# A clamp in two operations on POOL, low bits on POOL, and an order planned anew

## The chip, the cores and the metric

The kernel runs on one core of one Trainium2 chip. The metric is the device time of one execution in microseconds (us), lower is better. Engines are named as the profile names them: PE is TensorE, PEld its weight load, DVE is VectorE, ACT is ScalarE, POOL is GpSimd, SP the engine that issues most transfers.

## What is computed

Attention over 4 batches, 8 heads, 576 positions of 64 elements, and then two feed-forward layers over its 2304 rows of 512. In the attention a score that lies more than tau below its row's maximum is left out.

```python
scores = scale * np.matmul(q, k.transpose(0, 1, 3, 2))
thresh = np.max(scores, axis=-1, keepdims=True) - tau
scores = np.where(scores >= thresh, scores, -1000000000.0)
attn = np.exp(scores - max); attn = attn / (sum + 1e-09)
x = attn @ v                                  # rows of 512
x = (np.maximum(x @ w_in, 0.0) ** 2) @ w_out  # 512 -> 2048 -> 512
h = x @ w2_in
y = (h * np.tanh(log1p(exp(h)))) @ w2_out
```

The weights arrive as 64-bit floats, the rest as 32-bit.

## The kernel before, in words

The kernel is written as a list of small operations. Each has the engines on which it may run with an estimated time for each (S, A, P, V, T: SP's queue, ScalarE, POOL, VectorE, TensorE), the buffers that it reads and writes, and a due time. A planner (`Plan`) then walks through time, gives each operation an engine and a place in that engine's queue, and the kernel is emitted in this order. For an operation that may run on several engines, `forwards` compares for each engine the time when it would end there, plus a constant for the engine (`BIAS`). Several passes backwards and forwards set the due times anew (`fbi`). `PAR` holds the planner's settings: due times of the tiles (`blk`, `ahead`, `start`, `off`), which transfers may be issued by which engine (`won` for the weights, one entry for each layer), and how many of the weight places that stand empty at the start are lent to attention and to the conversion (`ex`, `exo`: `cr` raw weights, `cw` converted ones, `sc` scores, `raw` inputs, `pd` turned scores).

The work has three parts. Attention runs first, unit by unit: TensorE makes scores, VectorE evacuates them with their minimum or maximum (line 783), ScalarE takes the exponential (line 806), VectorE masks and sums (line 817) and normalises (lines 831, 834), TensorE multiplies with the values. The first layer takes nine tiles of 256 rows, each as soon as attention has them, and so runs among the attention. The second layer follows.

A weight is converted before its use, in 128 x 512 pieces, 32 for each layer: `load` brings the 64-bit words; `size` (line 462, ScalarE) takes the upper word's magnitude; `rest` (lines 470, 472) takes the top three bits of the lower word, on ScalarE by a multiplication and rounding or on VectorE by a shift; `clamp` (line 465, VectorE or POOL) limits the magnitude; `shift` (line 477) joins both; the sign comes back either by `sign` (line 483, VectorE) or by `factor` and `times` (lines 489, 492: ScalarE, then POOL or VectorE). Which way is taken, `sp` says: for layer 0 the first of a weight column's four pieces goes by `factor` and `times`. Then `to_hi` (line 511) rounds to TensorE's reduced 32-bit form and `to_lo` (line 521) subtracts to get the rest. The MLP's activations go through `to_hi` and `to_lo` as well.

The planner has a term for VectorE and POOL meeting: `port` is the time up to which one of them is occupied by an operation marked `two`, and the next such operation is made longer by 0.6 (VectorE) or 0.15 (POOL) of what is left.

Of the kernel before, what the change touches and what calls it, by code (L numbers as in the profile page):

```python
# [15 lines left out]
U32 = mybir.dt.uint32  # L16
# [11 lines left out]

PAR = dict(
    on=dict(),  # L30
    won=("S", "S"),
    land=1.8,
    lag=1.045,
    turns=("h", "s1"),
    kv=(("nat0", "V1"), ("f1", "nat1"), ("KT1", "f0"), ("V0", "KT0")),
    cd=(-103.359, 8.066, -43.099),
    urg=-3.138,
    rawt=19.607,
    kinds="dddd",
    cgen=0.081,  # L40
    split=(),
    ex=dict(cw=1, cr=22, raw=4, pd=2, sc=4),
    exo=("pd", "cw", "sc", "raw", "cr"),
    blk=list((22.378, 87.527, 172.036, 247.705, 353.772, 474.186, 575.438, 769.06, 852.156)),
    tb2=207.373,
    down2=-110.768,
    sp=(1, 0),
    off=(115.794, 85.638, 120.96, -226.354, 75.139, 25.769, -102.917, -5.246),
    ahead=(13.309, 135.862, 0.835, -119.128, 12.338, 42.57, 40.034, 91.863, 160.78, 84.376),
    start=-49.931,  # L50
    area=dict(sc=("x0", "x1"), hl=("x2",)),
    jobahead=19.218,
    fbi=8,
    stay=-23.036,
    kinds2="ssss",
)

# [21 lines left out]
class Plan:  # L79
# [3 lines left out]


    TABLE = 1.3
    BIAS = {"V": 2.329, "A": -28.964, "P": 2.606, "S": 0.46}
    SHARE = 0.8
    FIRST = 1.0
    TICK, ENTRY = 3.4133, 1.275

    def __init__(self):
# [105 lines left out]
    def forwards(self, succ):  # L197
# [3 lines left out]
        free = dict.fromkeys(engs, 0.0)  # L201
        queue = dict.fromkeys("APS", 0.0)
        cand = {e: {} for e in engs}
        port = 0.0
        table, half = None, False
        work = {}

# [12 lines left out]
        while count < len(ops):  # L220
            best = None
            for e in engs:
                c = cand[e]
                if not c:
                    continue
                t = max(free[e], min(c.values()))
                if best is not None and t >= best[0]:
                    continue
                now = sorted((ops[n].due, n) for n, at in c.items() if at <= t)
                pick = None  # L230
                for _, n in now:
                    o = ops[n]
                    if len(o.opts) > 1:
                        bias = self.BIAS
                        mine = t + o.opts[e] + bias[e]
                        better = False
                        for a, d in o.opts.items():
                            if a != e:
                                ahead = sum(
                                    ops[m].opts[a] for m, at in cand[a].items()  # L240
                                    if at <= t and ops[m].due < o.due and len(ops[m].opts) == 1
                                )
                                if max(free[a], cand[a][n]) + ahead + d + bias[a] < mine - 1e-9:
                                    better = True
                        if better:
                            continue
                    pick = n
                    break
                if pick is None:

                    later = [at for at in c.values() if at > t]
                    later += [f for f in free.values() if f > t]
                    if not later:
                        continue
                    free[e] = stop = min(later)
                    if best is None or stop < best[0]:
                        best = (stop, e, None)
                    continue
                if e == "A" and ops[pick].tab is not None and table is not None and table not in ops[pick].tab:
                    same = [n for _, n in now if ops[n].tab is None or table in ops[n].tab]  # L260
                    same = [n for n in same if ops[n].due < ops[pick].due + 4.0 and len(ops[n].opts) == 1]
                    if same:
                        pick = same[0]
                if e == "T" and ops[pick].half != half:
                    same = [n for _, n in now if ops[n].half == half and ops[n].due < ops[pick].due + PAR["stay"]]
                    if same:
                        pick = same[0]
                if best is None or t < best[0]:
                    best = (t, e, pick)
            t, e, pick = best  # L270
            if pick is None:
                continue
            o = ops[pick]
            for a in o.opts:
                cand[a].pop(pick, None)
            o.eng, o.start = e, t
            dur = o.opts[e]
            if o.load is None and (e == "P" or e == "V" and o.two):
                dur += (0.15 if e == "P" else 0.6) * max(0.0, port - t)
                port = max(port, t + dur)  # L280
            if e == "A" and o.tab is not None:
                if table is None or table not in o.tab:
                    dur += self.TABLE
                    table = o.tab[0]
            if e == "T":
                dur += 0.1 * (half and not o.half)
                half = o.half
            free[e] = t + dur if e != "T" else self.stream(work, t, dur)
            o.end = free[e]
            if o.load is not None:  # L290
                off, last, z = o.load
                t += PAR["land"] + (0.15 if e == "P" else 0.0) + (self.FIRST if t < 8.0 else 0.0)
                to = max(t, queue[e])
                other = max(f for a, f in queue.items() if a != e)
                z += min(z, max(0.0, other - to)) * self.SHARE
                o.end = queue[e] = max(t + off + last, to + z)
            count += 1
            for s in succ[pick]:
                left[s] -= 1
                if not left[s]:  # L300
                    offer(ops[s])
# [4 lines left out]
def attention_moe_moe_kernel(ctx: ExitStack, tc: tile.TileContext, q, k, v, tau, w1i, w1o, w2i, w2o, out):  # L306
    nc = tc.nc
# [55 lines left out]
    def rot(*places):  # L363
# [8 lines left out]
        "q1": (dict(S=0.75, P=0.8), 0.0, 0.4, 0.4), "q2": (dict(S=1.45, P=1.4), 0.62, 0.19, 0.65),  # L372
        "w": (dict(S=0.6, P=0.75, A=0.45), 0.0, 1.8, 1.75), "n3": (dict(S=2.3, P=2.0), 1.24, 0.9, 1.6),
        "n2": (dict(S=1.45, P=1.35), 0.62, 0.5, 1.4),
        "xs": (dict(S=0.72, P=0.65), 0.0, 0.36, 0.36), "tail": (dict(S=1.3, P=1.3), 0.6, 0.19, 0.38),
        "xl": (dict(S=0.63, P=0.56), 0.0, 0.55, 0.5), "x2": (dict(S=0.6, P=0.56), 0.0, 0.75, 0.7),
        "xr": (dict(S=0.45, P=0.56), 0.0, 0.64, 0.64), "out": (dict(S=0.45, A=0.45), 0.0, 0.65, 0.65),
        "out4": (dict(S=2.6), 1.8, 0.2, 0.8), "turn": (dict(S=1.55), 0.0, 1.3, 1.2),
# [45 lines left out]
    def weights(layer, kind, j, due, places, wplaces):  # L424
# [5 lines left out]
        for half in range(2):  # L430
# [23 lines left out]
            def lower(raw=raw):  # L454
                return raw()[:, :, 0]
# [6 lines left out]
                nc.scalar.activation(out=w(), in_=upper().bitcast(F32), func=AF.Abs, scale=W_SCALE)  # L462

            def clamp(e, w=w):
                VEC[e].tensor_scalar(out=w(), in0=w(), scalar1=W_MAX, scalar2=None, op0=ALU.min)


            def rest(e, lower=lower):
                if e == "A":
                    nc.scalar.activation(out=lower(), in_=lower().bitcast(U32), func=AF.Copy, scale=0.93 * 2.0 ** -29)  # L470
                else:
                    nc.vector.tensor_scalar(
                        out=lower(), in0=lower(), scalar1=29, scalar2=None, op0=ALU.logical_shift_right
                    )
# [18 lines left out]

            dma(load, "w", w=[raw], due=due - 12, on=PAR["won"][layer])
            op({"A": 0.56}, size, r=[raw], w=[w], due=due - 4)
            op({"A": 0.56, "V": 0.34}, rest, x=[raw], due=due - 3.5 + O_CV, two=True)
            op({"V": 0.34, "P": 1.45}, clamp, x=[w], due=due - 3 + O_CV, two=True)
            op({"V": 0.6}, shift, r=[raw], x=[w], due=due - 2 + O_CV, two=True)
            if 2 * kind + half < PAR["sp"][layer]:
                op({"A": 0.56}, factor, x=[raw], due=due - 1.9 + O_CV)  # L500
                op({"P": 1.24, "V": 0.6}, times, r=[raw], x=[w], due=due - 1.8 + O_CV, two=True)
            else:
                op({"V": 0.6}, sign, r=[raw], x=[w], due=due - 1.9 + O_CV, two=True)
            to_hi(w, hi, part, due - 1 + O_CV)
# [2 lines left out]
    def to_hi(src, dst, part, due):  # L507
# [6 lines left out]
            else:  # L514
                nc.vector.tensor_copy(out=o, in_=i)

        op({"A": 0.52, "V": 0.34, "P": 0.6}, fn, r=[src], w=[dst], due=due, two=True)

    def to_lo(src, hi, lo, part, due):
        def fn(e):  # L520
            VEC[e].tensor_tensor(out=part(lo), in0=src(), in1=f32(part(hi)), op=ALU.subtract)  # L521

        op({"V": 0.6, "P": 1.24}, fn, r=[src, hi], w=[lo], due=due, two=True)


    x_dr = [dbuf(f"xdr{n}", [128, 2, 512], F32) for n in range(NB)]
# [299 lines left out]
    def head(p, g, hh, u, ex, due):  # L826
# [19 lines left out]
            VEC[e].tensor_tensor(out=hl()[:, a:a + n], in0=ex()[:, z:z + n], in1=hl()[:, z:z + n], op=ALU.subtract)  # L846

        op({"A": 0.58, "V": 0.38}, high, r=[ex], w=[hl], due=due + 2.5 + O_HL, two=True)
        op({"V": 0.6, "P": 1.24}, lambda e: low(e, 640, 0, 512), r=[hl, ex], w=[hl], due=due + 3 + O_HL, two=True)
        op({"V": 0.14, "P": 0.3}, lambda e: low(e, 576, 512, 64), r=[hl, ex], w=[hl], due=due + 3 + O_HL, two=True)  # L850
        pt = sbuf(place("pt", "pt0", "pt1", "pt2"), [128, 9, 128], F16)
        transpose(pt, hl, [hl], [pt], due + 4 + O_HL)
# [317 lines left out]
    def second():  # L1170
# [10 lines left out]
        for i, n in enumerate((*range(NB - 2), NB - 1, NB - 2)):  # L1181
# [3 lines left out]
            for g in range(2):  # L1185
# [15 lines left out]
                    VEC[e].tensor_tensor(out=xo(), in0=xr(), in1=f32(xh()), op=ALU.subtract)  # L1201

                op({"A": 0.52, "V": 0.34, "P": 0.66}, hi, r=[xr], w=[xh], due=blkd - 6, two=True)
                op({"V": 0.6, "P": 1.24}, lo, r=[xr, xh], w=[xo], due=blkd - 5, two=True)
                hs.append(xh)
                os_.append(xo)
            x = View(hs), View(os_)
# [171 lines left out]
```

## Time and profile before

| what | us |
|---|---|
| median of 3 runs | 1057.93 |
| the three runs | 1058.05, 1057.93, 1055.40 |
| the profiled execution's own time | 1057.58 |
| its span, first to last instruction | 1055.8 |
| TensorE busy in the span | 1012.6 |
| VectorE, ScalarE, POOL busy | 742.9, 786.8, 119.6 |

The span is what the rows below divide up. The profile's line numbers are those of the code above. Busy times of TensorE are modelled, as its instructions overlap; idle time of an engine matters only where that engine is the bound.

### The profile page before, as it was taken

The numbers are of one execution on the slowest core, as the hardware profiler recorded it, in microseconds if no ns is written. First come the engines' busy times: TensorE is split into PE (matmuls) and PEld (weight loads), VectorE is DVE, ScalarE is ACT, GpSimd is POOL, SyncE is SP. The second block draws the span as 40 slices with busy tenths as digits, with TensorE's granted clock in tenths as the row PEclk, the third lists the DMA queues.
The fourth block names the chain that finished last, engine by engine and source line by source line (L and its number), as shares of the span: only waits on it lengthen the run. The fifth ranks groups of instructions, "written<-read, shape, count | busy, mean of one in ns | idle before, by whom it ended". The sixth has DMA issues, their size and how long they took to land. (4 is left out here: it accounts for less than half of the span.)

```text
span 1055.8 us, 24074 instructions
## 1 busy us (share of the span) xinstructions
PE 1012.6 (96%) x9484; PEld 915.7 (87%) x9484; DVE 742.9 (70%) x1675; ACT 786.8 (75%) x1301; POOL 119.6 (11%) x132
## 2 busy tenths in 40 slices
PE   6998789799999999999999999899999999999998
PEld 4665478688989898998999999899999999999997
DVE  5999899999888998897574149875454444464443
ACT  5989789787776877776685369978777676596774
POOL 1451333310111111121000000000000000000000
PEclk9999889999999999999999999999999999999999
DMA  9532479889989888976863014410100000000000
GB/s 301 149 125 65 121 160 207 168 155 173 174 153 170 155 185 160 173 156 116 188 212 122 31 37 165 140 55 27 36 14 32 20 21 21 31 30 1 20 21 20
DMA packets 240146, 113.78 MB, mean 108 GB/s; under 512 B 202784, under 2 KB 221728, under 8 KB 240032
## 3 DMA queue, kind: packets, MB, share of 16 engines
q1 hardware_dynamic: 239744, 111.71, 45.9%
q8 instruction: 74, 1.21, 0.5%
q10 hardware_dynamic: 288, 0.52, 0.1%
q14 instruction: 40, 0.33, 0.1%
HBM read 58.33 MB, written 14.16 MB: 69 GB/s over the span
## 5 line engine op out<-in xcount | busy, mean ns | idle before, releaser
L392 PE MATMUL s<-KT,area 64*128 64x64 f16 (+6 forms) x880 | 87.6, 323 | 6.0 <-DVE wi7l L783 1.9
L1175 ACT ACT_TABLE_LOAD x70 | 89.8, 1283 | 1.2
L521 DVE TENSOR_TENSOR gl<-r,gh 128x512 fp32r<-128x512 f32 x83 | 57.0, 687 | 47.1 <-ACT gh L511 45.4
L511 ACT ACTIVATE gh<-r 128x512 fp32r<-128x512 f32 x90 | 56.4, 626 | 31.0 <-PE acc L392 29.0
L806 ACT ACTIVATE e<-area,m 128x576 f32<-128x576 f32 x91 | 68.2, 768 | 15.0 <-DVE hl L846 5.4
L817 DVE SCALAR_TENSOR_TENSOR e<-area,n,e 128x576 f32<-128x576 f32 x91 | 72.6, 814 | 8.0 <-ACT e L806 7.4
L783 DVE TENSOR_SCALAR_CACHE_REDUCE area<-s,c 128x576 f32<-128x576 f32 x91 | 72.1, 812 | 7.3 <-PE s L392 6.7
L1127 ACT ACTIVATE r<-h 128x512 f32<-128x512 f32 x72 | 42.6, 592 | 35.6 <-PE h L392 31.0
L1223 DVE TENSOR_SCALAR area<-area 128x512 f32<-128x512 f32 x37 | 15.7, 426 | 76.0 <-ACT area L1179 75.9
L392 PE MATMUL small<-V,pt 128*128 128x64 f16 (+1 forms) x1680 | 66.4, 196 | 1.7 <-ACT xt L975 0.8
L392 PEld LDWEIGHTS <-pt 128*128 128x128 f16 (+1 forms) x1680 | 56.7, 102 | 10.9 <-issue 7.1
L846 DVE TENSOR_TENSOR hl<-e,hl 128x512 f16<-128x512 f32 (+1 forms) x101 | 61.6, 617 | 4.3 <-ACT hl L841 4.3
L841 ACT ACTIVATE hl<-e 128x576 f16<-128x576 f32 x77 | 51.5, 676 | 13.3 <-DVE e L817 6.0
L846 POOL TENSOR_TENSOR hl<-e,hl 128x64 f16<-128x64 f32 (+1 forms) x53 | 31.0, 587 | 167.5 <-ACT hl L841 158.5
L1179 ACT ACTIVATE area<-area 128x512 f32<-128x512 f32 x74 | 46.1, 630 | 0.5
L1134 ACT ACTIVATE r<-r 128x512 f32<-128x512 f32 x72 | 45.2, 627 | 0.9
L392 PEld LDWEIGHTS <-area 64*128 64x128 f16 (+1 forms) x720 | 23.7, 98 | 24.3 <-issue 3.6
L1179 ACT ACTIVATE area<-s 128x512 f32<-128x512 f32 x24 | 14.3, 596 | 40.2 <-PE s L392 40.0
L521 DVE TENSOR_TENSOR gl<-e,gh 128x512 fp32r<-128x512 f32 x36 | 24.8, 689 | 20.2 <-ACT gh L511 20.1
L470 ACT ACTIVATE area<-area 128x512 int32<-128x512 uint32 x51 | 38.9, 769 | 0.0
L511 ACT ACTIVATE gh<-e 128x512 fp32r<-128x512 f32 x36 | 22.5, 626 | 21.3 <-PE acc L392 21.2
L1249 DVE TENSOR_TENSOR r<-s,area 128x512 f32<-128x512 f32 x23 | 15.9, 691 | 30.4 <-ACT area L1179 30.4
(776 smaller groups left out, 4116.2 us busy)
## 6 DMA issues: line engine op xcount, KB each, us to landing
area<-in_moe_w_in_dram SPq DMA_DIRECT2D x27, 512.0 KB, 4.6
area<-in_moe_w_out_dram SPq DMA_DIRECT2D x24, 512.0 KB, 4.1
xl<-xdr SPq DMA_DIRECT2D x36, 128.0 KB, 2.9
x2dr<-stg SPq DMA_DIRECT2D x18, 256.0 KB, 2.5
xdr<-xs SPq DMA_DIRECT2D x32, 128.0 KB, 2.3
f<-in_v_dram SPq DMA_DIRECT2D x12, 256.0 KB, 3.1
f<-in_k_dram SPq DMA_DIRECT2D x22, 128.0 KB, 3.8
area<-in_q_dram SPq DMA_DIRECT2D x20, 128.0 KB, 2.8
```

The lines of the kernel that those rows point to most:

```text
L392: nc.tensor.matmul(o, l, r, start=start, stop=stop, skip_group_check=True)
L511: nc.scalar.activation(out=o, in_=i, func=AF.Copy)
L521: VEC[e].tensor_tensor(out=part(lo), in0=src(), in1=f32(part(hi)), op=ALU.subtract)
L783: nc.vector.tensor_scalar(out=sc(), in0=s()[:, 0:576], scalar1=c()[:, 3:4], scalar2=None, op0=ALU.mult, op1=ALU.min, accum_out=m()[:, i:i ...
L806: lambda e: nc.scalar.activation(out=ex(), in_=sc(), func=AF.Exp, bias=m()[:, i:i + 1], scale=-1.0),
L817: nc.vector.scalar_tensor_tensor(out=ex(), in0=sc(), scalar=nt()[:, i:i + 1], in1=ex(), op0=ALU.is_le, op1=ALU.mult, accum_out=l()[:, 0, u ...
L841: nc.scalar.activation(out=hl()[:, 0:576], in_=ex(), func=AF.Copy)
L846: VEC[e].tensor_tensor(out=hl()[:, a:a + n], in0=ex()[:, z:z + n], in1=hl()[:, z:z + n], op=ALU.subtract)
L1127: nc.scalar.activation(out=halves(r()), in_=turned_out(ph()), func=AF.Relu)
L1134: nc.scalar.activation(out=r(), in_=r(), func=AF.Square)
L1175: nc.scalar.preload_act_table_set({"ln": "natural_log_exp_and_others", "sig": "sigmoid_and_others"}[table])
L1179: nc.scalar.activation(out=out, in_=in_, func=func, **kw)
```

## The change

`clamp` gets a form of its own on POOL, with a second operation that changes nothing (a maximum with 0 of a magnitude). `rest` may run on POOL too, as a multiplication with an addition of 0. The planner's costs for POOL change: the clamp from 1.45 to 0.71, the subtractions from 1.24 to 1.33, the rounding from 0.6 to 0.68. The planner's term for VectorE and POOL is written anew: a POOL operation takes a share of VectorE's time (0.57, or 0.3 if it is shorter than 0.8 us), also from an operation of VectorE that has begun already. All settings are chosen anew, and with them the order of all instructions. `sp` becomes 0 for layer 0, so `factor` and `times` no longer occur. The weights' loads of layer 0 may be issued by ScalarE. With `ex` and `exo`, one place that attention's scores had goes to raw weights. What the operations compute stays as it was.

```diff
 PAR = dict(
-    won=("S", "S"),
+    won=("SA", "S"),
-    lag=1.045,
+    lag=0.886,
-    cd=(-103.359, 8.066, -43.099),
-    urg=-3.138,
+    cd=(-120.141, 6.917, 7.077),
+    urg=-8.108,
-    ex=dict(cw=1, cr=22, raw=4, pd=2, sc=4),
-    exo=("pd", "cw", "sc", "raw", "cr"),
-    blk=list((22.378, 87.527, 172.036, 247.705, 353.772, 474.186, 575.438, 769.06, 852.156)),
+    ex=dict(cw=1, cr=14, raw=4, pd=2, sc=3),
+    exo=("cw", "sc", "pd", "raw", "cr"),
+    blk=list((3.899, 78.791, 166.909, 241.414, 350.2, 463.155, 565.113, 791.555, 811.314)),
-    sp=(1, 0),
+    sp=(0, 0),
...
-    BIAS = {"V": 2.329, "A": -28.964, "P": 2.606, "S": 0.46}
+    BIAS = {"V": 2.417, "A": -9.314, "P": 2.639, "S": 0.46}
+    PORT = (0.57, 0.3)
...
-            if o.load is None and (e == "P" or e == "V" and o.two):
-                dur += (0.15 if e == "P" else 0.6) * max(0.0, port - t)
-                port = max(port, t + dur)
+            if o.load is None and e == "P":
+                share = self.PORT[dur < 0.8]
+                left_v = port["V"][0] - t
+                if left_v > 0:
+                    dur += 0.15 * min(dur, left_v)
+                    more = min(left_v * share / (1 - share), dur * share)
+                    free["V"] += more
+                    port["V"] = (port["V"][0] + more, 0.0)
+                port["P"] = (t + dur, share)
+            elif o.load is None and e == "V" and o.two:
+                left_p, share = port["P"][0] - t, port["P"][1]
+                if left_p > 0:
+                    dur = min(dur / (1 - share), dur + left_p * share)
+                port["V"] = (t + dur, 0.0)
...
             def clamp(e, w=w):
-                VEC[e].tensor_scalar(out=w(), in0=w(), scalar1=W_MAX, scalar2=None, op0=ALU.min)
+                if e == "P":
+                    nc.gpsimd.tensor_scalar(out=w(), in0=w(), scalar1=W_MAX, scalar2=0.0, op0=ALU.min, op1=ALU.max)
+                else:
+                    nc.vector.tensor_scalar(out=w(), in0=w(), scalar1=W_MAX, scalar2=None, op0=ALU.min)
...
+                elif e == "P":
+                    nc.gpsimd.tensor_scalar(
+                        out=lower(), in0=lower().bitcast(U32), scalar1=0.93 * 2.0 ** -29, scalar2=0.0,
+                        op0=ALU.mult, op1=ALU.add,
+                    )
...
-            op({"A": 0.56, "V": 0.34}, rest, x=[raw], due=due - 3.5 + O_CV, two=True)
-            op({"V": 0.34, "P": 1.45}, clamp, x=[w], due=due - 3 + O_CV, two=True)
+            op({"A": 0.56, "V": 0.34, "P": 0.71}, rest, x=[raw], due=due - 3.5 + O_CV, two=True)
+            op({"V": 0.34, "P": 0.71}, clamp, x=[w], due=due - 3 + O_CV, two=True)
...
-        op({"V": 0.6, "P": 1.24}, fn, r=[src, hi], w=[lo], due=due, two=True)
+        op({"V": 0.6, "P": 1.33}, fn, r=[src, hi], w=[lo], due=due, two=True)
```

## Rows read from the trace of the kernel before

**Rows 1.** The page: the span.

```profile
span 1055.8 us, 24074 instructions
```

**Rows 2.** Busy us by stage: PE, PEld, DVE, ACT, POOL; granted clock, DMA share, GB/s.

```profile
0.00:26.00 26.00, 17.68 (x130) 12.55 (x132) 13.21 (x30) 15.06 (x26) 3.62 (x9) 1.00 0.92 300
26.00:106.00 80.00, 71.06 (x656) 50.04 (x653) 75.88 (x196) 71.90 (x145) 31.47 (x21) 0.98 0.39 114
106.00:158.00 52.00, 43.15 (x406) 32.47 (x405) 48.89 (x116) 40.82 (x74) 19.09 (x17) 0.84 0.62 140
158.00:211.00 53.00, 47.05 (x527) 41.84 (x527) 53.00 (x119) 43.26 (x76) 18.96 (x16) 0.97 0.89 188
211.00:634.00 423.00, 419.76 (x4893) 388.77 (x4890) 324.19 (x835) 301.95 (x516) 45.11 (x69) 1.00 0.72 148
634.00:739.00 105.00, 102.05 (x772) 98.13 (x771) 80.51 (x136) 92.62 (x149) 1.34 (x1) 0.98 0.29 96
739.00:1030.00 291.00, 291.00 (x1993) 273.33 (x1993) 139.06 (x235) 208.57 (x303) 0.00 (x0) 1.00 0.07 23
1030.00:1055.80 25.80, 20.87 (x120) 18.59 (x118) 8.18 (x13) 12.62 (x18) 0.00 (x0) 0.99 0.06 21
```

**Rows 3.** What TensorE waited for, 0 to 211 us: total, times, longest.

```profile
PE acc L889 <- DVE e L817: 4.2, 5, 1.3
PE small L392 <- DVE l L831: 3.9, 1, 3.9
...
PE s L392 <- DVE wi7l L783: 3.0, 4, 1.7
```

**Rows 4.** Busy time of line 465 (clamp) alone by stage: DVE, POOL.

```profile
0.00:211.00 211.00, 9.52 (x19) 21.40 (x13) 0.94 0.64 162
211.00:634.00 423.00, 7.18 (x17) 0.00 (x0) 1.00 0.72 148
634.00:739.00 105.00, 6.27 (x15) 0.00 (x0) 0.98 0.29 96
```

**Rows 5.** Line 470 (low bits) alone: ACT.

```profile
0.00:211.00 211.00, 21.98 (x32) 0.94 0.64 162
```

**Rows 6.** Line 489 (factor) alone: ACT.

```profile
0.00:211.00 211.00, 5.63 (x8) 0.94 0.64 162
```

**Rows 7.** Line 492 (multiplication) alone: DVE, POOL.

```profile
0.00:211.00 211.00, 2.80 (x4) 6.63 (x4) 0.94 0.64 162
```

**Rows 8.** Line 483 (sign) alone: DVE.

```profile
0.00:211.00 211.00, 19.27 (x24) 0.94 0.64 162
```

**Rows 9.** Line 521 (subtraction of the rounded part) alone: DVE, POOL.

```profile
0.00:211.00 211.00, 10.40 (x16) 34.38 (x24) 0.94 0.64 162
```

**Rows 10.** Timeline of POOL, 43.2 to 51.5 us: start, duration.

```profile
43.88 1.28 POOL L521 TENSOR_TENSOR wi1l<-wi7h,wi1h 128x512 fp32r<-128x512 f32 x1 [6.88 <-ACT wi1h L511]
49.00 1.49 POOL L465 TENSOR_SCALAR wi7h<-wi7h 128x512 f32<-128x512 f32 x1 [3.83 <-ACT wi7h L462]
50.45 1.49 POOL L465 TENSOR_SCALAR stg<-stg 128x512 f32<-128x512 f32 x1
```

**Rows 11.** Timeline of VectorE in the same stretch.

```profile
43.99 1.79 DVE L817 SCALAR_TENSOR_TENSOR e<-wo6h,n,e 128x576 f32<-128x576 f32 x1
...
48.99 1.23 DVE L817 SCALAR_TENSOR_TENSOR e<-wi6h,n,e 128x576 f32<-128x576 f32 x1
...
50.89 0.81 DVE L817 SCALAR_TENSOR_TENSOR e<-wi7l,n,e 128x576 f32<-128x576 f32 x1
```

**Rows 12.** Groups of POOL's instructions, shapes apart.

```profile
L604 POOL TENSOR_SCALAR f<-f,cv 128x640 f32<-128x640 f32 x1 | 1.9, 1897 | 0.0
...
masks.py:199 POOL TENSOR_SCALAR_AFFINE_SELECT ident<-ident 128x128 f32<-128x128 f32 x1 | 0.3, 294 | 0.1
L409 POOL MEMSET ones<- 128x128 f32 x1 | 0.2, 207 | 0.0
...
L1361 POOL MEMSET const-float32-0.0<- 128x1 f32 x1 | 0.1, 99 | 0.2 <-issue 0.2
```

More of the change, by code (lines that the diff above doesn't have):

```diff
@@ L30 @@
     on=dict(),
-    won=("S", "S"),
+    won=("SA", "S"),
     land=1.8,
-    lag=1.045,
+    lag=0.886,
     turns=("h", "s1"),
     kv=(("nat0", "V1"), ("f1", "nat1"), ("KT1", "f0"), ("V0", "KT0")),
-    cd=(-103.359, 8.066, -43.099),
-    urg=-3.138,
-    rawt=19.607,
+    cd=(-120.141, 6.917, 7.077),
+    urg=-8.108,
+    rawt=12.027,
     kinds="dddd",
-    cgen=0.081,
+    cgen=1.313,
     split=(),
-    ex=dict(cw=1, cr=22, raw=4, pd=2, sc=4),
-    exo=("pd", "cw", "sc", "raw", "cr"),
-    blk=list((22.378, 87.527, 172.036, 247.705, 353.772, 474.186, 575.438, 769.06, 852.156)),
-    tb2=207.373,
-    down2=-110.768,
-    sp=(1, 0),
-    off=(115.794, 85.638, 120.96, -226.354, 75.139, 25.769, -102.917, -5.246),
-    ahead=(13.309, 135.862, 0.835, -119.128, 12.338, 42.57, 40.034, 91.863, 160.78, 84.376),
-    start=-49.931,
+    ex=dict(cw=1, cr=14, raw=4, pd=2, sc=3),
+    exo=("cw", "sc", "pd", "raw", "cr"),
+    blk=list((3.899, 78.791, 166.909, 241.414, 350.2, 463.155, 565.113, 791.555, 811.314)),
+    tb2=275.975,
+    down2=-155.23,
+    sp=(0, 0),
+    off=(128.724, 97.6, 116.366, -141.171, 63.45, 21.057, -181.555, -13.003),
+    ahead=(12.828, 109.297, -7.851, -101.613, 11.358, 163.606, 14.023, 24.714, 212.091, 227.813),
+    start=-91.594,
     area=dict(sc=("x0", "x1"), hl=("x2",)),
-    jobahead=19.218,
+    jobahead=18.886,
     fbi=8,
-    stay=-23.036,
+    stay=-27.053,
     kinds2="ssss",
@@ L203, in forwards @@
         cand = {e: {} for e in engs}
-        port = 0.0
+        port = {"V": (0.0, 0.0), "P": (0.0, 0.0)}
         table, half = None, False
@@ L374, in attention_moe_moe_kernel @@
         "n2": (dict(S=1.45, P=1.35), 0.62, 0.5, 1.4),
-        "xs": (dict(S=0.72, P=0.65), 0.0, 0.36, 0.36), "tail": (dict(S=1.3, P=1.3), 0.6, 0.19, 0.38),
+        "xs": (dict(S=0.72, P=0.65), 0.0, 0.36, 0.36), "tail": (dict(S=1.6, P=1.3), 0.6, 0.19, 0.38),
         "xl": (dict(S=0.63, P=0.56), 0.0, 0.55, 0.5), "x2": (dict(S=0.6, P=0.56), 0.0, 0.75, 0.7),
@@ L500, in weights @@
                 op({"A": 0.56}, factor, x=[raw], due=due - 1.9 + O_CV)
-                op({"P": 1.24, "V": 0.6}, times, r=[raw], x=[w], due=due - 1.8 + O_CV, two=True)
+                op({"P": 1.33, "V": 0.6}, times, r=[raw], x=[w], due=due - 1.8 + O_CV, two=True)
             else:
@@ L515, in fn @@
                 nc.vector.tensor_copy(out=o, in_=i)
-        op({"A": 0.52, "V": 0.34, "P": 0.6}, fn, r=[src], w=[dst], due=due, two=True)
+        op({"A": 0.52, "V": 0.34, "P": 0.68}, fn, r=[src], w=[dst], due=due, two=True)
     def to_lo(src, hi, lo, part, due):
@@ L848, in head @@
         op({"A": 0.58, "V": 0.38}, high, r=[ex], w=[hl], due=due + 2.5 + O_HL, two=True)
-        op({"V": 0.6, "P": 1.24}, lambda e: low(e, 640, 0, 512), r=[hl, ex], w=[hl], due=due + 3 + O_HL, two=True)
+        op({"V": 0.6, "P": 1.33}, lambda e: low(e, 640, 0, 512), r=[hl, ex], w=[hl], due=due + 3 + O_HL, two=True)
         op({"V": 0.14, "P": 0.3}, lambda e: low(e, 576, 512, 64), r=[hl, ex], w=[hl], due=due + 3 + O_HL, two=True)
@@ L1203, in second @@
                 op({"A": 0.52, "V": 0.34, "P": 0.66}, hi, r=[xr], w=[xh], due=blkd - 6, two=True)
-                op({"V": 0.6, "P": 1.24}, lo, r=[xr, xh], w=[xo], due=blkd - 5, two=True)
+                op({"V": 0.6, "P": 1.33}, lo, r=[xr, xh], w=[xo], due=blkd - 5, two=True)
                 hs.append(xh)
```

## The prediction

> **What bounds the kernel now.** I read four views, from coarse to fine.
>
> First the page's head: the profiled execution spans 1055.8 us [rows 1]. Its own time is 1057.58 us, so 1.78 us lie around the span. The median of the three runs shown is 1057.93 us, 0.35 us more; the sum below is made against 1057.58.
>
> Then busy time by stage [rows 2]. The reader is to see two different kernels there. From 211 to 1030 us TensorE is busy for 419.76 of 423, 102.05 of 105 and 291 of 291 us: it is the bound, and the change gives it no instruction more or less. Before 211 us it isn't. TensorE is busy for 17.68 of 26, 71.06 of 80, 43.15 of 52 and 47.05 of 53 us, together 178.9, so 32.1 us are idle; 8.3 of these are the start, before data is there. VectorE in the same rows works 75.88 of 80, 48.89 of 52 and 53.00 of 53 us from 26 us on: 96%. ScalarE has 71.90, 40.82 and 43.26, which is 156.0 of 185 us or 84%. So VectorE bounds the first fifth, and TensorE's work is fixed behind it: a microsecond of VectorE time that goes away before 211 us can end the kernel one microsecond earlier, up to the 23.7 us that TensorE idles between 26 and 211. The granted clock falls there as well, to 0.84 between 106 and 158 us [rows 2], and comes back to full once TensorE is fed. It costs little while TensorE waits for VectorE anyway, and I put nothing on it.
>
> Third, whom TensorE waits for before 211 us: the masking of the scores (line 817), 4.2 us, the normalising sums (line 831), 3.9 us in one wait, the scores' evacuation (line 783), 3.0 us [rows 3]. All are VectorE's; the waits are attention's, not the weights'. So the weight conversion hurts by taking VectorE's time, not by being late itself.
>
> Fourth, the lines that the change touches, each alone by stage [rows 4 to 9], what POOL does to VectorE [rows 10, 11], and what short POOL operations cost [rows 12].
>
> **The change part by part, for the stretch before 211 us.**
>
> *The price of a short POOL operation.* The one-operation clamp takes POOL 1.49 us undisturbed [rows 10]. No row shows a two-operation form over 512 elements. From below: a memset takes 99 ns for one element and 207 ns for 128 [rows 12], so 512 cost about 0.10 + 4 x 0.108 = 0.53 us. The affine select over 128 takes 294 ns [rows 12], which gives 0.10 + 4 x 0.195 = 0.88. From above: the single multiply-and-add over 640 elements took 1897 ns [rows 12], so 1.52 us for 512. The small constants come from the same engine alone, the 640 ran beside VectorE's work; I take the middle of the lower two, 0.71 us, which is also the cost that the diff writes into its table. The Trainium skill, GPSIMD Engine Reference, section Elementwise — side-by-side cycle accounting, gives 1.03 cycles per element for a body of up to two operations; an estimate from it and the page's 1.2 GHz is 0.44 us and dispatch. That page doesn't tell the one-operation form apart, and the 1.49 us of the row disagrees with it, so it moves nothing here.
>
> *What POOL costs VectorE.* Two neighbouring pictures. POOL's two-input subtraction at 43.88 us (1.28 us) [rows 10] lies beside a masking on VectorE that begins at 43.99 and takes 1.79 us, where an undisturbed one takes 0.81 [rows 11]: 0.98 us lost, it runs only when POOL is through. POOL's one-input clamp at 49.00 (1.49 us) has a masking of 1.23 us beside it, 0.42 lost; the clamp at 50.45 has one of 0.81 begun at 50.89, nothing lost. So a two-input POOL operation costs VectorE 0.98, a one-input one between 0 and 0.42; I take the mean, 0.21. The Trainium skill, SBUF — State Buffer, section SBUF: two separate sides, has it otherwise: the port pair that the two engines share is locked for a whole instruction, and the other engine blocks fully. The subtraction agrees with that (0.98 of 1.28), the clamp at 50.45 does not (0 of 1.49). What it would make of the time is rival 2.
>
> (a) Clamps that go from VectorE to POOL. VectorE runs 19 clamps here in 9.52 us, 0.50 each, POOL 13 in 21.40 [rows 4]. At half the price the planner will give POOL more. Bounds: none, and all 19 at no loss, 9.5 us. I take 10: 10 x (0.50 - 0.21) = 2.9 us gained.
>
> (b) The 13 that POOL has already become half as long. They cost VectorE 13 x 0.21 = 2.7 us now; at 0.71 for 1.49, half of that: 1.3 us gained (bounds 0 and 2.7).
>
> (c) The parameter sp goes from 1 to 0 for the first layer: 8 factors leave ScalarE, 5.63 us [rows 6], and 8 multiplications go, 4 on VectorE in 2.80 us and 4 on POOL in 6.63 us [rows 7]; 8 sign operations come, VectorE's only, at 19.27 / 24 = 0.80 us [rows 8]. Four of these replace four alike. The other four add 3.2 us to VectorE, and four two-input POOL operations of 0.98 us loss go, 3.9 us: 0.7 us gained (bounds: 3.2 lost, if the four met nothing on VectorE, and 0.7).
>
> (d) The low bits on POOL. All 32 are ScalarE's now, 21.98 us [rows 5]. ScalarE isn't the bound here, so what it loses is worth nothing by itself; its slack of 29 us hides it. Each one that moves costs VectorE 0.21. The planner still prefers ScalarE strongly (a bias of -9.3 against 2.6), so I take 6: 1.3 us lost (bounds: 0, and 32 x 0.42 = 13.4 lost).
>
> (e) The new order. 24 subtractions of low parts run on POOL here, in 34.38 us, 16 on VectorE in 10.40, 0.65 each [rows 9]. One on POOL costs VectorE 0.98 and saves 0.65: 0.33 lost by having it there. A planner that charges VectorE for it may place them where VectorE runs scores out of PSUM, or leave them on VectorE. All 24 are worth 7.9 us; I take half, 4.0 gained. The order also changes what cannot be priced so: one score tile less at the start, one raw buffer more, all the due times; and up to 32 weight loads may leave SP's queue for ScalarE's, whose 29 us of slack hide their issue, and would wait there behind exponentials if ScalarE ran full. Downward I bound that with the largest single wait of the order before, 3.9 us [rows 3], happening twice more: 7.8 lost.
>
> Later stages count for nothing. The second layer's 17 + 15 clamps on VectorE [rows 4] lie under TensorE's 98 to 99%; if that cover were gone, each is worth 7.18 / 17 = 0.42 us. The 3 us that TensorE idles between 634 and 739 us are the entry into the second layer, the 4.9 after 1030 us the end of the last tile [rows 2]; I leave both as they are, and the first, were a clamp on its way, bounds the gain there.
>
> Sum: 2.9 + 1.3 + 0.7 - 1.3 + 4.0 = 7.6 us. 1057.58 - 7.6 = 1050.0 us, 0.7% less.
>
> **The rivals.**
>
> 1. *No change.* POOL is only 73.1 of 211 us busy [rows 2]; what the short clamps free there is filled with more subtractions, the kind that costs VectorE 0.33 net each. Twelve more eat 4 us, and (e) brings nothing: 7.6 - 4.0 - 4.0 = -0.4, so 1058. For it: the planner's choice goes by who ends first, not by VectorE's loss. Against: the loss now moves VectorE's free time in the plan.
>
> 2. *Slower: the low bits go to POOL in bulk and stall VectorE.* With 20 on POOL at 0.42, 8.4 us are lost, (a) shrinks to 10 x 0.08 = 0.8, (b) and (e) fall away, (c) stays: -6.9 us, 1064.5. It decides from 12 on, where 12 x 0.42 exceeds (a) to (c), 4.9. For it: the masking at 48.99 us; against: the one at 50.89 us [rows 11], and the bias for ScalarE. By the lock rule of the Trainium skill, named above, a VectorE operation would lose up to the whole 0.71 us, and this rival would decide from 7 on.
>
> 3. *Slower: the two-operation form isn't shorter* (1.52 by the 640-element row, worse perhaps with unsigned integers in and out). Then 29 POOL operations planned at 0.71 end 0.8 us late each; VectorE takes its queue in order, so the shift that waits for them holds the scores behind it. If half fall on slack, 29 x 0.8 x 0.5 = 11.6 lost against 4.0 of (e): 1065. Before, none of TensorE's three largest waits names POOL.
>
> **How the numbers follow.** Within 0.3% of the median (3.2 us) no change can be told. Forecast 0.56, rival 1 0.20, rival 2 0.12, rival 3 0.12; so faster 0.56, same 0.20, slower 0.24. The likeliest case alone runs from 1043, with (a) whole and (e) nearly so, to 1054.5. The whole range leaves a tenth at each end: 1041, since more would need most of the 23.7 us, to 1065, rivals 2 and 3.
>
> **What would show it.** Two-operation clamps on POOL near 0.7 us, more than 13 before 211 us, VectorE's busy time there below 191.0 us, and TensorE's idle time there from 32 to about 24 us: right. POOL's subtractions above 24: rival 1. Line 470 mostly on POOL and masking of 1.2 us beside it: rival 2. POOL near 1.5 us and VectorE waiting for POOL: rival 3. The prediction fails altogether if the new order moves TensorE's waits to transfers, or opens idle time after 211 us.

## The result and the profile after

The changed kernel takes 1065.86 us (median of 4 runs, 1063.62 to 1067.49), the kernel before 1057.0 us beside it (4 runs). The ratio is 1.0084, with a 95% interval of 1.006 to 1.0108: slower by some 9 us. The forecast was 1050.0 us, the range 1041 to 1065, so the time lies 0.9 us above the range. That it comes so near is luck: the upper end stood for rivals 2 and 3, and neither is what happened.

The profiled execution took 1065.80 us and spans 1064.0. Busy time by stage of the changed kernel, columns as in [rows 2]:

```profile
0.00:26.00 26.00, 4.84 (x40) 3.76 (x40) 0.74 (x4) 2.37 (x3) 0.85 (x7) 1.00 0.97 293
26.00:106.00 80.00, 69.09 (x613) 49.11 (x614) 73.19 (x177) 69.67 (x136) 24.56 (x25) 1.00 0.32 101
106.00:158.00 52.00, 43.09 (x335) 29.94 (x333) 48.27 (x127) 43.16 (x84) 14.56 (x14) 0.79 0.57 130
158.00:211.00 53.00, 51.69 (x612) 47.21 (x612) 50.72 (x125) 45.50 (x78) 15.64 (x18) 0.98 0.92 191
211.00:634.00 423.00, 421.29 (x4944) 390.41 (x4943) 332.74 (x857) 301.67 (x513) 39.99 (x64) 1.00 0.73 149
634.00:739.00 105.00, 100.69 (x801) 96.88 (x800) 81.97 (x136) 95.41 (x155) 6.29 (x6) 1.00 0.32 106
1030.00:1064.00 34.00, 29.11 (x172) 26.20 (x170) 13.44 (x23) 19.33 (x28) 0.00 (x0) 1.00 0.08 23
```

Set these against [rows 2]. TensorE's idle time before 26 us rises from 8.3 to 21.2 us. From 26 to 211 us it falls, from 23.7 to 21.1 (185 less 69.09, 43.09 and 51.69). Then come 1.7 for 3.2 us up to 634, 4.3 for 2.9 up to 739, and 4.9 for 4.9 at the end. So the 10.0 us more of idle time are the first 26 us (12.8) less what the rest won. (The span grows by 8.2 us only, because TensorE's modelled busy time is 1.8 us shorter.) In that first row VectorE works 0.74 us and ScalarE 2.37, where they worked 13.21 and 15.06: everything stands still.

What TensorE waited for, in the whole changed kernel: in total, times, longest. Below it are the same three waits in the kernel before.

```profile
PE s L404 <- ACT area L738: 20.4, 1, 20.4
PE s L404 <- DMA wi6h<-in_k_dram: 5.0, 1, 5.0
...
PE s L404 <- DMA wi6l<-in_q_dram: 1.1, 1, 1.1
```

```profile
PE s L392 <- DMA wi6l<-in_k_dram: 3.6, 1, 3.6
...
PE s L392 <- DMA wo5h<-in_q_dram: 1.7, 1, 1.7
...
PE s L392 <- ACT area L718: 1.6, 1, 1.6
```

One wait of 20.4 us is larger than all the gains that the prediction listed. It is for ScalarE, for the evacuation of the first turned inputs (line 738, line 718 before). For the transfers of these inputs TensorE waits 6.1 us in all, where it waited 5.3. ScalarE's own timeline says why it is late; rows with ACTq are transfers that its queue issues, the number after the start is the issue's length.

```profile
0.74 1.04 ACTq L448 DMA_DIRECT2D area<-in_moe_w_in_dram  x2
5.50 0.35 ACTq L456 DMA_DIRECT2D xh<-in_moe_w_out_dram  x1
7.78 0.39 ACTq L448 DMA_DIRECT2D wi5h<-in_moe_w_in_dram  x1
8.84 0.35 ACTq L456 DMA_DIRECT2D xo<-in_moe_w_out_dram  x1
11.96 0.42 ACTq L448 DMA_DIRECT2D wi5l<-in_moe_w_in_dram  x1
15.71 0.44 ACTq L448 DMA_DIRECT2D wi4h<-in_moe_w_in_dram  x1
16.55 0.39 ACTq L448 DMA_DIRECT2D wi4l<-in_moe_w_in_dram  x1
19.15 0.35 ACTq L456 DMA_DIRECT2D wo4h<-in_moe_w_out_dram  x1
23.24 0.35 ACTq L456 DMA_DIRECT2D wo4l<-in_moe_w_out_dram  x1
23.62 1.28 ACT L474 ACT_TABLE_LOAD   x1 [23.62 <-DMA wi6l<-in_q_dram]
24.91 0.66 ACT L474 ACTIVATE stg<-area 128x512 f32<-128x512 f32 x1
```

ScalarE's first instruction proper, a table load, begins at 23.62 us, and its first activation at 24.91; in the kernel before that was at 6.89:

```profile
6.89 0.66 ACT L462 ACTIVATE stg<-area 128x512 f32<-128x512 f32 x1 [4.89 <-DMA area<-in_moe_w_in_dram]
```

Ahead of it in the same queue stand ten weight loads. Their issues take 0.35 to 0.52 us each, 4.1 us together; 18.8 of the 23.6 us are gaps between them. The program's list of ScalarE's instructions tells what the gaps are (x2 stands for the first two loads):

```
1 L448 DMA area<-in_moe_w_in_dram 128x2x512 x2
2 L456 DMA xh<-in_moe_w_out_dram 128x1024 [waits DMAHW0_49]
3 L448 DMA wi5h<-in_moe_w_in_dram 128x2x512 [waits DMAHW3_49]
4 L456 DMA xo<-in_moe_w_out_dram 128x1024 [waits DMAHW6_49]
...
9 L456 DMA wo4l<-in_moe_w_out_dram 128x1024 [waits DMAHW0_49]
10 L474 ACT_TABLE_LOAD
```

Each load from the third on waits for one of eight completion counters, which SP's transfers use in turn as well. A load whose buffer has long been free still waits there until an earlier transfer of the same counter has landed, and with it everything behind it in ScalarE's queue. The trace shows the counters too, and when each was reached: the eight issues from the third on begin 0.02 us after the last part of the earlier transfer on their counter has landed (at 5.48, 7.76, 8.82, 11.94, 15.69, 16.53, 19.13 and 23.22 us).

### The profile page after: what moved, and what is told of

Read it like the earlier page. It is cut to its first block, busy times and chain, and to the rows that moved or that the text cites. A ratio compares the mean times of both kernels' runs of the same rounds, so it can differ in the third digit from the quotient of the medians.

```text
span 1064.0 us, 24055 instructions
## 1 busy us (share of the span) xinstructions
PE 1010.8 (95%) x9484; PEld 916.6 (86%) x9484; DVE 738.4 (69%) x1675; ACT 784.5 (74%) x1293; POOL 101.9 (10%) x131
## 4 chain that ended last, share of the span: by engine, by line
PE 69%; ACT 4%; DVE 3%; issue 2%; DMA 1%; POOL 0%; DVEq 0%; POOLq 0%; ACTq 0%
PE acc L404 30%; PE h L404 17%; PE s L404 15%; PE small L404 7%; ACT area L1199 1%; PE s L1102 1%; DMA x2dr<-stg 1%; DMA area<-nat 0%; ACT L1195 0%; ACT area L485 0%; DVE area L803 0%; DVE gl L541 0%; ACT gh L531 0%; ACT nat L474 0%; ACT hl L1199 0%
## 5 line engine op out<-in xcount | busy, mean ns | idle before, releaser
L404 PE MATMUL s<-KT,area 64*128 64x64 f16 (+6 forms) x880 | 89.5, 326 | 24.6 <-ACT area L738 20.4
L837 DVE SCALAR_TENSOR_TENSOR e<-area,n,e 128x576 f32<-128x576 f32 x91 | 74.8, 837 | 5.1 <-ACT e L826 4.0
L866 DVE TENSOR_TENSOR hl<-e,hl 128x512 f16<-128x512 f32 (+1 forms) x106 | 64.1, 611 | 7.2 <-ACT hl L861 7.1
L404 PEld LDWEIGHTS s<-KT,area 64*128 64x128 f32 (+1 forms) x160 | 18.0, 202 | 38.9 <-ACT area L738 20.6
L866 POOL TENSOR_TENSOR hl<-e,hl 128x64 f16<-128x64 f32 (+1 forms) x48 | 26.1, 546 | 172.3 <-ACT hl L861 159.7
```

What stands on the lines that cost most here:

```text
L404: nc.tensor.matmul(o, l, r, start=start, stop=stop, skip_group_check=True)
L837: nc.vector.scalar_tensor_tensor(out=ex(), in0=sc(), scalar=nt()[:, i:i + 1], in1=ex(), op0=ALU.is_le, op1=ALU.mult, accum_out=l()[:, 0, u ...
```

## The experiments

The queue theory: the ten loads, by waiting in ScalarE's queue, hold back its first activation and with it TensorE, and that is the loss. Its rival, the transfer theory: early weights crowd out attention's first inputs on the transfer engines, whoever issues them. A second question is what is left of the prediction's 7.6 us once the start is out of the way. Ratios are to the kernel before on the same chip.

**e1.** The ten loads on SP.

```diff
         for n in seq:
             o = plan.ops[n]
-            o.fn(o.eng)
+            early = o.load is not None and o.eng == "A" and o.start < 5.0
+            o.fn("S" if early else o.eng)
```

> The changed kernel with every engine's order kept, but the ten weight loads that ScalarE's queue holds ahead of its first activation are issued by SP, each at its place in the planned sequence. Queue theory (the loads wait in ScalarE's queue for earlier transfers and hold the first activation until 23.6 us): the first activation comes before 12 us, the 20.4 us wait of TensorE is gone, TensorE's idle time before 26 us falls from 21.2 to 9 to 13 us, the time from 1065.9 to 1052 to 1058. Transfer theory (the weights crowd out the first inputs wherever they are issued, so TensorE starts late all the same): 1062 or more, with TensorE's long wait now on transfers.

1055.26 us, ratio 0.9988 (0.9973 to 1.0003); spans 1051.9. The first activation comes at 6.08 us and the 20.4 us wait is gone. First 26 us, and TensorE's longest wait in them:

```profile
0.00:26.00 26.00, 10.24 (x75) 7.53 (x77) 12.11 (x24) 12.78 (x20) 4.38 (x11) 1.00 0.87 299
```

```profile
PE s L404 <- DMA wi6l<-in_q_dram: 8.5, 1, 8.5
```

The queue theory holds for some 10 us (ratio 0.9988 for 1.0084). But TensorE still idles 15.8 us here, more than the 9 to 13 expected: on SP five weight loads stand ahead of the second input (q), and TensorE waits for that. That wait comes with this run's own edit: in the changed kernel the one for the same input is 1.1 us.

**e2.** As e1, the same loads on POOL's queue.

```diff
-            o.fn(o.eng)
+            o.fn("P" if early else o.eng)
```

> The same ten loads issued by POOL at their places, so SP's queue holds what it held in the changed kernel and the weights may still go as early. Queue theory: ScalarE starts before 12 us, 1052 to 1059 (POOL makes the identity matrix behind four loads, which may cost TensorE a few us at the start). Transfer theory: as early weights crowd the inputs as before, 1062 or more.

1060.49 us, ratio 1.0038 (1.0022 to 1.0054): above the queue theory's figure and below the other's. ScalarE's first activation comes at 7.14 us, as the queue theory says, yet TensorE has other waits. Three of them:

```profile
PE s L404 <- ACT area L738: 6.7, 1, 6.7
PE s L404 <- DMA wi6l<-in_q_dram: 6.0, 1, 6.0
PE s L404 <- POOL ident masks.py:199: 4.8, 1, 4.8
```

The identity matrix, which POOL makes behind four loads, accounts for 4.8 us. The q input, issued at 2.68 us as in the changed kernel, lands 10.5 us later where it took 5.9 there: POOL issues its first nine loads by 8.2 us, without such gaps. That is what the transfer theory expects of early weights, so it describes a part of this run; in the changed kernel, whose loads are spread out by the gaps, it doesn't show. The run tells that a queue's head is a poor place for loads on POOL too, and it doesn't tell the theories apart by its time.

**e3.** A dose between: e1's condition leaves the first four loads with ScalarE.

```diff
+            early = o.load is not None and o.eng == "A" and 1.5 < o.start < 5.0
+            o.fn("S" if early else o.eng)
```

> A dose between: of the ten loads the first four stay in ScalarE's queue ahead of its first activation, six go to SP. Queue theory: the first activation comes when the fourth load is issued, 8 to 11 us instead of 24.9, and the time is within 3 us of the run with none there. Transfer theory: 1062 or more, as in the other two.

1054.21 us, ratio 0.9988 (0.9973 to 1.0004). ScalarE's queue:

```profile
0.73 1.04 ACTq L448 DMA_DIRECT2D area<-in_moe_w_in_dram  x2
1.80 0.49 ACTq L456 DMA_DIRECT2D xh<-in_moe_w_out_dram  x1
8.09 0.38 ACTq L448 DMA_DIRECT2D wi5h<-in_moe_w_in_dram  x1
8.49 1.28 ACT L474 ACT_TABLE_LOAD   x1 [8.49 <-DMA wi6h<-in_k_dram]
9.79 0.66 ACT L474 ACTIVATE stg<-area 128x512 f32<-128x512 f32 x1
```

The first three loads go without a pause, the fourth waits from 2.3 to 8.09 us, and the first activation follows at 9.79: four loads cost ScalarE 3 us against 6.89, ten cost 18. And TensorE waits for its inputs then anyway, so the time is that of e1.

**e7.** The reverse: the kernel before, its own order, only its first nine weight loads issued by ScalarE ahead of everything else.

```diff
+            loads.add(len(plan.ops))
...
+    early = sorted((o.start, o.n) for o in plan.ops if o.n in loads)[:9]
+    at = {n: 0.45 * i + 0.01 for i, (_, n) in enumerate(early)}
...
-        for n in seq:
+        for n in sorted(range(len(plan.ops)), key=lambda n: (at.get(n, plan.ops[n].start), n)):
             o = plan.ops[n]
-            o.fn(o.eng)
+            o.fn("A" if n in at else o.eng)
```

> The kernel before with nothing changed but this: its first nine weight loads are issued by ScalarE ahead of its first activation. Queue theory: the first activation comes at 18 to 25 us instead of 6.9, TensorE idles 10 us or more longer before 26 us, and the time is 8 to 14 us above before: 1064 to 1070. Rival, that the changed kernel's loss lies in its other settings: within 3 us of before.

1067.47 us, ratio 1.0103 (1.008 to 1.0125): the changed kernel's loss, without any other part of the change. First 26 us, TensorE's longest wait, and parts of ScalarE's timeline:

```profile
0.00:26.00 26.00, 8.00 (x56) 5.71 (x58) 5.43 (x14) 7.65 (x12) 2.34 (x8) 1.00 0.88 292
```

```profile
PE s L392 <- ACT area L719: 11.1, 1, 11.1
```

```profile
0.71 1.04 ACTq L436 DMA_DIRECT2D area<-in_moe_w_in_dram  x2
...
16.76 0.39 ACTq L436 DMA_DIRECT2D wi4l<-in_moe_w_in_dram  x1
17.18 1.28 ACT L462 ACT_TABLE_LOAD   x1 [17.18 <-DMA wo4h<-in_moe_w_in_dram]
18.47 0.66 ACT L462 ACTIVATE stg<-area 128x512 f32<-128x512 f32 x1
```

TensorE idles 18.0 us there for 8.3 before, 9.7 more, just under the 10 expected. With e1 and e3, which take the loads away, the queue theory is shown from both sides.

**e6.** The changed kernel with the loads offered to SP alone; the planner makes its order anew with that.

```diff
-    won=("SA", "S"),
+    won=("S", "S"),
```

> The changed kernel with one setting put back: weight loads of layer 0 may be issued by SP alone, and the planner makes its order with that. Queue theory: ScalarE's first activation before 12 us, TensorE's 20.4 us wait gone; the other settings weren't chosen for this, so 1048 to 1060. Rival (the other settings are what costs the time): 1063 or more.

1055.40 us, ratio 0.9980 (0.996 to 1.0). TensorE idles 8.0 us before 26 us, as in the kernel before. All the other settings together cost nothing; they gain 0.4% at most.

**e4.** The kernel before, its order untouched; its 13 clamps on POOL in the two-operation form.

> The kernel before with its order untouched; only its 13 clamps on POOL take the two-operation form. By the prediction's term (b) POOL's clamps fall from 1.49 to about 0.63 us and VectorE loses half as much beside them: 1.3 us gained, 1055 to 1057. Rival: the shorter form holds the shared port and stalls VectorE more than the long one did: 1 to 4 us slower than before, with maskings of over 1 us beside the clamps.

1054.39 us, ratio 0.9972 (0.9959 to 0.9985): about 3 us faster, more than the 1.3 of term (b). The 13 clamps alone (line 466 in this kernel) and then all engines, 0 to 211 us:

```profile
0.00:211.00 211.00, 9.36 (x13) 0.94 0.64 162
```

```profile
0.00:211.00 211.00, 178.81 (x1714) 136.96 (x1716) 189.85 (x458) 171.06 (x318) 61.30 (x62) 0.94 0.64 162
```

POOL's time for them falls from 21.40 [rows 4] to 9.36 us, and VectorE is busy for 1.1 us less than the 191.0 of before, which is term (b). The rest of the gain isn't explained by it: in the profiled execution TensorE idles 0.8 us less than before from 26 to 211 us, but 2.3 us less from 211 to 634, where POOL made no clamp before [rows 4]. The rival, that the short form stalls VectorE more, is out.

**e5.** The changed kernel's order, the ten loads on SP and set among the first inputs about as in the kernel before.

```diff
+    early = [o.n for o in plan.ops if o.load is not None and o.eng == "A" and o.start < 5.0]
...
+    at = dict(zip(early, (0.5, 3.0, 3.1, 5.1, 5.0, 7.0, 10.0, 10.1, 13.0, 13.1)))
...
+        for n in sorted(range(len(plan.ops)), key=lambda n: (at.get(n, plan.ops[n].start), n)):
+            o.fn("S" if n in at else o.eng)
```

> The changed kernel with the ten early weight loads on SP as in e1, but set among the attention's first inputs in about the sequence of the kernel before, so that TensorE's second input is no longer behind five weight loads (in e1 TensorE waited 8.5 us for it). If the new order is worth what the prediction gave it and only the start spoilt it: TensorE's idle time before 26 us at most 11 us (e1: 15.8, before: 8.3), and 1047 to 1052. Rival, the new order is worth nothing and what e1 gained back is only the start: no better than e1, 1054 to 1057.

1054.39 us, ratio 0.9981 (0.9965 to 0.9997): faster than before, but at the rival's figure. By stage:

```profile
0.00:26.00 26.00, 14.92 (x104) 11.26 (x105) 14.69 (x31) 15.56 (x28) 4.05 (x11) 0.97 0.91 284
26.00:106.00 80.00, 70.17 (x645) 50.72 (x643) 73.59 (x188) 69.36 (x136) 24.45 (x24) 0.95 0.44 128
106.00:158.00 52.00, 46.54 (x424) 35.32 (x425) 48.03 (x127) 41.96 (x80) 14.08 (x15) 0.83 0.66 149
158.00:211.00 53.00, 50.27 (x596) 45.27 (x593) 51.67 (x126) 46.10 (x80) 19.73 (x18) 1.00 0.83 172
```

From 26 to 211 us TensorE idles 18.0 us, 5.7 fewer than before; before 26 us it idles 11.1, which is 2.8 more and as expected about the bound of 11.

**e8.** As e5, with POOL's clamps in the one-operation form again.

```diff
-                    nc.gpsimd.tensor_scalar(out=w(), in0=w(), scalar1=W_MAX, scalar2=0.0, op0=ALU.min, op1=ALU.max)
+                    nc.gpsimd.tensor_scalar(out=w(), in0=w(), scalar1=W_MAX, scalar2=None, op0=ALU.min)
```

> As e5, but POOL's clamps in the one-operation form of the kernel before (1.49 us), in the same order. 24 of them run before 211 us and were planned at 0.71 us. By the prediction's rival 3 each comes 0.8 us late and VectorE takes its queue in order: 5 to 12 us slower than e5. If POOL's slack hides them: within 2 us of e5.

1055.71 us, ratio 0.9996 (0.998 to 1.0012). It is 1.5 parts in a thousand above e5, and the intervals overlap: by the expectation's measure, POOL's slack hides most of 24 clamps that come late.

**e9.** As e5, and the evacuations of the first two turned inputs ahead of the next weight pieces in ScalarE's queue.

```diff
+    at.update({2: 6.7, 3: 6.8, 5: 8.4, 6: 8.5})
```

> As e5, and the evacuations of the first two turned inputs stand in ScalarE's queue ahead of the next weight pieces, as in the kernel before; in e5 they waited behind pieces that land at 9.5 us and later, and TensorE lost 3.4 us to it. If the start is a plain loss and the rest of the new order is worth 6 us (e5 idled 18.0 us from 26 to 211, the kernel before 23.7): TensorE busy 17 us or more before 26 us (e5 14.9), and 1049 to 1053. Rival, the time won at the start is lost again behind VectorE: no better than e5, 1054 to 1056.

1052.38 us, ratio 0.9946 (0.9924 to 0.9967). The time is where the first theory had it, the mechanism is not: TensorE is busy for 14.65 us before 26 us, no more than in e5. It waits now for VectorE to evacuate scores, in total, times, longest:

```profile
PE s L404 <- DVE wo7l L803: 3.2, 2, 3.0
```

The profiled execution spans 1051.5 us, that of e5 1052.1, and the intervals of the two overlap. What e9 adds to e5 isn't settled.

**e10.** As e4, and every subtraction that POOL makes is VectorE's, at its place in the order.

```diff
+        lows.add(len(plan.ops))
         op({"V": 0.6, "P": 1.24}, fn, r=[src, hi], w=[lo], due=due, two=True)
...
-            o.fn(o.eng)
+            o.fn("V" if n in lows else o.eng)
```

> As e4 (the kernel before with the two-operation clamp), and all subtractions that POOL makes (24 before 211 us, 3 after) are VectorE's, each at its place in the order. By the prediction's price in (e) one on POOL costs VectorE 0.98 us of stall and saves 0.65 of work, so VectorE gains 7.9 us and TensorE's idle time from 26 to 211 us falls by some of that: 1047 to 1052. Rival: most subtractions on POOL meet operations that read scores from PSUM and cost nothing, so the move adds up to 24 x 0.65 = 15.6 us to VectorE: 1057 to 1066.

1051.17 us, ratio 0.9938 (0.9918 to 0.9959), the lowest of all, though its interval overlaps that of e9 and touches that of e4. All engines, and line 526 (the subtraction) alone, 0 to 211 us:

```profile
0.00:211.00 211.00, 181.03 (x1734) 138.91 (x1735) 191.46 (x487) 173.39 (x321) 26.58 (x38) 0.95 0.65 163
```

```profile
0.00:211.00 211.00, 28.21 (x40) 0.95 0.65 163
```

VectorE makes 40 subtractions here for 16 in [rows 9], 28.21 us for 10.40, and its busy time in this stretch is only 1.6 us more than in e4. So 24 subtractions, 17.8 us of work, replaced 16.2 us of stalls: 0.68 us for each that POOL made, not 0.98. The stretch holds five more of VectorE's other instructions here than in e4, so the whole span is the cleaner count: 27 subtractions move, VectorE's subtractions cost 17.9 us more (0.66 each), and it is busy for 740.4 us instead of 741.8. That gives 0.71 us of stall for each. The time lies where the price of 0.98 had it (1047 to 1052), but the 7.9 us that VectorE was to gain by that price aren't there.

**e11.** As e9, with POOL's subtractions on VectorE, by the same edit as in e10.

> As e9, and all of POOL's subtractions are VectorE's. By the price in (e), as in e10, 3 to 8 us less than e9. If the new order had placed POOL's subtractions where they cost VectorE less than 0.65 us each: slower than e9.

1054.52 us, ratio 0.9972 (0.996 to 0.9984), at or above e9. In the new order the move brings nothing. VectorE's subtractions over the whole span, in e9 (line 541, with POOL's behind) and here (line 543):

```profile
0.00:1051.50 1051.50, 121.96 (x178) 40.97 (x30) 0.98 0.47 108
```

```profile
0.00:1051.80 1051.80, 142.86 (x208) 0.99 0.47 108
```

The 30 that move are 20.9 us of work, and VectorE's busy time rises from 739.0 to 743.5 us: each had cost 0.55 us of stall on POOL and costs 0.70 of work on VectorE. So the new order had set POOL's subtractions where they cost VectorE less, as the expectation has it. The timelines say where: before 211 us they run beside line 803, which reads scores out of PSUM, for 16.9 of their 34.0 us in e9, and beside the masking (line 837) for 3.9; in the kernel before, for 11.7 and 9.5 of 34.4 us.

## Why the prediction was wrong

**The step that failed** is the last part of (e): up to 32 weight loads may leave SP's queue for ScalarE's, "whose 29 us of slack hide their issue". Slack is an average over 26 to 211 us. The loads were not spread over it: ten stand at the head of the queue at time 0, when nothing is behind schedule and nothing hides them. And the issues were taken for work, which they are for 4.1 us only, while each can also wait, and the queue waits with it: the first activation came 18.0 us later. The prediction asked what would delay the loads (exponentials ahead of them) and not what the loads would delay. The question to be asked of an instruction that changes its queue, who stands behind it, was left out for these. The bound of 7.8 us for what "cannot be priced" was too small as well: the loss at the start is 12.8 us of TensorE's idle time. The planner has the same gap: it gives a load on ScalarE 0.45 us and knows no counters.

The start was set aside earlier still. The prediction took its 8.3 us of idle time as given, "before data is there", and of TensorE's waits it named the first, second and fourth and said "All are VectorE's". The third, 3.6 us for the first input's transfer (its row stands with the result, above), is the start's own, and the sign that TensorE hung on the head of the queues there. The prediction's own sign of failing, waits that move to transfers, came true in the form that ScalarE waits for transfers and TensorE for ScalarE.

The Trainium skill, Perfetto Trace Analysis, section DMA Instruction — HWDGE (DVE, Sync), says that the reported start of such an issue is the moment its semaphores are satisfied, so the wait ahead of it isn't drawn. This trace agrees: ten issues of 4.1 us together, and 18.8 us of gaps in which the queue seems empty. The Trainium skill, DMA: Bandwidth & Descriptors, section Issuing engines are not separate DMA queues, says that issuing from several engines saves only the sequencer's time to start a transfer. The runs agree here: with all loads on SP, e6 is 10 us faster than the changed kernel.

**What bounds the kernel** held from 26 us on: the differences after 211 us cancel to 0.2 us, and 26 to 211 us gave idle time back. In the first 26 us the bound was ScalarE's queue. (TensorE's cover for the later clamps was 97 to 99%, not 98 to 99%.) VectorE's busy time before 211 us is 172.9 us, under the 191.0 that was to be a sign of being right, but mostly because it stood still at the start (e5, without that, has 188.0); such a sign needs the idle time beside it.

**Price of the short form.** Held: 0.71 forecast, 0.63 to 0.76 as the medians of the two large groups, 0.84 as the mean of all. All 29 clamps on POOL are of two operations; the two groups, shortest, median, longest in ns:

```profile
L478 POOL TENSOR_SCALAR stg<-stg x18: 612/634/1276, 26.8 to 708.9; 128x512 f32<-128x512 f32 x18
...
L478 POOL TENSOR_SCALAR wo7h<-wo7h x7: 613/763/1140, 36.1 to 165.9; 128x512 f32<-128x512 f32 x7
```

**(a)** Held in count. Lines 478 (POOL's clamp), 480 (VectorE's) and 541 (subtractions: VectorE, POOL) alone before 211 us:

```profile
0.00:211.00 211.00, 19.32 (x24) 0.94 0.61 155
```

```profile
0.00:211.00 211.00, 3.35 (x8) 0.94 0.61 155
```

```profile
0.00:211.00 211.00, 12.06 (x14) 31.70 (x23) 0.94 0.61 155
```

POOL makes 24 clamps, 11 more than before (10 forecast), VectorE 8 in 3.35 us instead of 19 in 9.52.

**(b)** Held for VectorE: 1.3 us forecast, 1.1 us in e4. The time gained there is larger, 0.15 to 0.41% or 1.6 to 4.3 us, and where the rest comes from is open.

**(c)** As forecast in kind: no factor and no multiplication are left, and 8 signs more are VectorE's. Not tried alone.

**(d)** Not used: line 487 occurs nowhere in the trace, all 64 low bits stay with ScalarE. I had 6, worth 1.3 us. Rival 2 is out with it.

**(e), the subtractions.** 23 on POOL for 24: the order didn't move them off POOL. The other way that the prediction gave, to place them where VectorE reads scores from PSUM, it took: 0.55 us of stall each in the new order (e11) for 0.71 in the old (e10), an estimate from one pair of traces each. The price was too high: in the old order 0.68 to 0.71 of stall stand against 0.66 to 0.74 of work, no net loss on average. My 0.98 was one pair of rows, and there the masking didn't run "only when POOL is through": it ends at 45.78 us, 0.62 us after the subtraction, and takes 0.81 alone, so a part of it ran beside it. This also sizes the lock rule of the Trainium skill (SBUF — State Buffer, section SBUF: two separate sides), by which the engine that comes second blocks fully for the whole instruction of the other: a subtraction takes POOL 1.43 us and costs VectorE half of that on average.

**What is left without the start**: e5 and e9 run at 0.9981 and 0.9946, 2 to 6 us under the kernel before, for the 7.6 forecast. The sum counted VectorE's time; over the whole span that falls from 742.9 to 738.9 and 739.0 us, by about half of the 7.6. So the direction of the sum is shown, at a quarter to three quarters of its size in time. How the rest divides among its terms isn't: (b) is some 1 us, (d) none, (a) and (c) weren't tried alone. The form alone in the old order (e4) is worth as much as e5 has in all, so nothing here shows that the new order makes the kernel faster than the old.

**The rivals.** Rival 1 (no change) describes e1 and nearly e6, though not by its mechanism. Rival 3 had the time right (1065) for a reason that is shown wrong: the form is shorter, and e8 prices its absence at some 1.5 us where I had 11.6.

**Open**: whether e10 gains over e4 at all, as the intervals touch, and why, when VectorE's busy time is only 1.4 us shorter. In the profiled executions TensorE idles 1.3 us less in e10 than in e4 before 26 us, 0.9 less from 26 to 211 and 0.9 more from 211 to 634. That the maskings are more even without stalls is only an argument.

## What to carry to other kernels

When an edit moves a transfer to another engine's queue, price what stands behind it there: an issue of 0.4 us can wait for a counter or a buffer, and an engine's queue waits with it. Look for this at time 0 first, where a planner finds the queue empty and slack over a long stretch says nothing. A gap between issues on a compute engine's queue, ahead of its first instruction, is the sign to look for in the trace.

## What the runs showed of the hardware that was not expected

The one-operation clamp takes POOL 1.49 us over 512 elements, the same clamp with a second, idle operation 0.61 to 0.63: more work in the instruction, less than half the time. The single multiply-and-add with a scale from a tile still took 1.89 us over 640 elements in e4, so two operations as such don't seem to make the form short; what does, no run here tells. (That one is a single instruction, and beside VectorE's work.)
